# A planned kernel of linear attention and an MLP: code-block boundaries in the planner, early products and norms off VectorE, some K transposed by DMA

## The chip, the cores and the metric

The kernel runs on one core of one Trainium2 chip. TensorE (PE) multiplies matrices; its weight loads are shown as a row of their own (PEld). VectorE (DVE), ScalarE (ACT) and GpSimd (POOL) work on elements, SyncE (SP) issues most of the DMAs, and 16 DMA engines move the data. The metric is the device time of one execution in microseconds (us), less is better. Times are medians over executions; the profile is of one execution.

## What is computed

The reference is a linear attention with a delta rule over 768 steps for 4 x 8 heads of width 48, and then an MLP with a tanh gelu on the 3072 tokens.

```
k_n = k / (norm(k, axis=-1) + 1e-06)
for t in range(S):
    y[:, :, t] = einsum('bhd,bhde->bhe', q[:, :, t], state)
    v_old = einsum('bhde,bhd->bhe', state, k_n[:, :, t])
    state = state + beta_t * einsum('bhd,bhe->bhde', k_n[:, :, t], v[:, :, t] - v_old)
x = y.transpose(0, 2, 1, 3).reshape(3072, 384)
out = gelu_tanh(x @ w_in) @ w_out          # 384 -> 2048 -> 384
```

## The kernel before

**A planner writes the order.** The kernel doesn't loop over instructions in a fixed order. Each piece of work is declared with `op(...)`: which engines can do it and what it should cost there, what it reads and writes, a priority (less is more urgent), the number `nm` of matmuls in it, and for a DMA its semaphore. `Plan.schedule` (L110) then simulates the engines with these costs and picks, for each engine, the next operation: one that could start within `NEAR` of the engine's free time goes before one that is late, and among these the most urgent. The result is five fixed instruction streams (`emit`, L268). An engine executes its stream strictly in order and waits with semaphores, so where real times differ from planned ones, an engine waits in its place. SP's and POOL's DMAs stand in their streams like all else.

**Code blocks.** PE's stream has some 11,000 instructions, a weight load and a matmul for each of 5446 matmuls. They are fetched in blocks of 256. Class `Fetch` (L32) models that: each time PE's count passes a multiple of 256, the next block must have arrived, which takes TIME = 3.7 us after the crossing before, or BUSY = 6.5 in the first 50 us. A PE operation that would stall longer than `SLACK` counts as late by the rest (L194 to L199).

**Stages.** The 768 steps are cut into 12 chunks of 64, two chunks to a unit. Heads lie in pairs on 128 partitions, 16 pairs side by side. For a chunk:
- `prep` (L670) squares K (`sq`), sums it (`ss`, L682, a VectorE reduce), and makes 1/norm (`rn`); `prep2` (L739) scales K to `Kn` on POOL or VectorE, transposes it on PE with 8 matmuls against an identity (L762) and copies the result to `KQT` (L773). `prepq` (L715) does the like for Q (L728).
- `gram` (L775) multiplies K with K and with Q. ScalarE copies the first to `G`; VectorE multiplies the second by the decay mask `mD` into `DT` (L800).
- `own` (L804) and `blocks` (L834), once a unit: a triangular 16x16 inverse by a recurrence of 14 steps, each a product into `tmp` and a sum into `Yf` (L872, L876). For unit 0 it runs on VectorE, for later units on POOL. `XW`, `TB` (L891), then in `inverse` (L896) `WB` and `DI` (L917), `ET`, and three `TT` steps widen it to 64x64.
- `state` (L979): R, U, the new state S and the outputs of a chunk, copied to `x4` (L1076).

`mlp` (L1082) works on tiles: tile 0 is chunk 0, tile 1 is chunk 1, the others are two chunks each. SP moves some rows of x first, six small DMAs a tile (not for tile 0). The first layer's results go through gelu on ScalarE to `gT`, the second layer's to `osb` and out by SP. Only banks 6 and 7 of PSUM are used by MLP work until the last tile.

**Loads.** K, V and Q chunks are loaded on SP (`load`, L565). The weights are loaded on POOL's queue: W1 and W4 (the parts of w_in) after chunk 2 of K has landed, W2 (w_out) after the first Qs. `O` (L357) holds the priorities.

Of the kernel before, what the change touches and what calls it, by code (L numbers as in the profile page):

```python
# [17 lines left out]
URGENT = -100.0  # L18
EARLY_T, MARGIN = 55.0, (2.0, 1.0, 0.2)
# [12 lines left out]
class Fetch:  # L32

    BLOCK, TIME, BUSY, BUSY_T = 256, 3.7, 6.5, 50.0

    def __init__(self):
        self.pos, self.ready = 0, 0.0

    def run(self, t, cost, n, keep=False):
        pos, ready = self.pos, self.ready  # L40
        per = cost / n
        while n:
            k = min(self.BLOCK - pos % self.BLOCK, n)
            t += k * per
            pos += k
            n -= k
            if pos % self.BLOCK == 0:
                t = max(t, ready)
                ready = t + (self.BUSY if t < self.BUSY_T else self.TIME)
        if keep:  # L50
            self.pos, self.ready = pos, ready
        return t
# [7 lines left out]
class Plan:  # L60
# [49 lines left out]
    def schedule(self):  # L110
# [51 lines left out]
        while n_left:  # L162
            pick = None
            for e in ENGINES:
# [3 lines left out]
                for i in ready[e]:  # L168
# [34 lines left out]
                    far = late > (NEAR[e] if o.prio > URGENT else 0.12)  # L203
# [19 lines left out]
            if o.dma:  # L223
                arrival = o.end + 1.5
                if e == "pool":
                    w_free = max(arrival, w_free) + o.bw
                    o.lat = w_free + 0.5 - o.end
                    for p in queued:
                        if p.end + p.lat - 0.5 > arrival:
                            p.lat += o.bw  # L230
                    if dma_free > arrival:
                        dma_free += o.bw
                        dep_cache.clear()
                    else:
                        dma_free = w_free
                else:
                    dma_free = max(arrival, dma_free) + o.bw
                    o.lat = dma_free + 0.5 - o.end
                    queued.append(o)
# [28 lines left out]
    def emit(self):  # L268
# [64 lines left out]
        with nc.Block() as blk:  # L333
# [19 lines left out]
GATE = 2  # L353
XQ_, OQ_ = "sp", "sp"
BURST, SLACK = 0.6, 0.15
NEAR = dict(pe=0.2, dve=0, act=0.2, pool=0.5, sp=0.0)
O = dict(step=79.0, prepq=-76.8, prep=-99.5, prep0=-83.8, prep1=-94.9, prep2=-81.3, gram=-57.3, w2=-63.2,  # L357
         prepq0=-58.2, dt0=-84.0, dtb=-43.9, dt=-67.0, own=-153.9, own0=-86.2, blk0=-78.6, inv0=-95.4,
         st0=-103.2, own1=-46.4, blk=-48.3, blk1=-29.7, invb=-46.3, stb=-46.9, inv=-22.2, st=24.3,
         x=23.8, mlpa=-100, m1=1.6, m2=53.1, outs=300, ldq=-122.7, ldk=-121.8, ldv=-92.0)  # L360
# [50 lines left out]
def bass_deltanet__then__act_gelu_tanh_kernel(  # L411
# [25 lines left out]
    with nc.allow_non_contiguous_dma("head rows"), nc.allow_low_precision("bf16 matmuls"):  # L437
# [127 lines left out]
        def load(nm, c, pr):  # L565
# [11 lines left out]
            for a in range(2):  # L577
                op({"sp": 0.75}, {"sp": f_dma(t[s][64 * a:64 * a + 64, :, :], sv[a, C * c:C * c + C, :, :])},
                   reads=after, writes=[f"{nm}{s}_{a}"], prio=pr, dma=f"d_{nm}{c}", bw=1.27)
# [6 lines left out]
        def load_w1(kt, pr):  # L586
            after = ["kf2_0", "kf2_1"]
# [9 lines left out]
        def load_w1x(pr):  # L597
            after = ["vf1_0", "vf1_1"]
# [13 lines left out]
        def load_w4(pr):  # L612
            op({"pool": 0.9}, {"pool": lambda e: e.memset(W4, 0.0)}, writes=W4S, prio=-96)
            after = ["kf2_0", "kf2_1"]
# [9 lines left out]
        def load_w2(j, pr):  # L624
            op({"pool": 0.8}, {"pool": f_dma(W2[:, 4 * j:4 * j + 4, :], w2v[:, 4 * j:4 * j + 4, :])},
               reads=["qf_0", "qf_1", "qf_2", "qf_3"],
               writes=[f"W2{j}"], prio=pr, dma=f"d_W2{j}", bw=2.5)
            bulk.append([f"W2{j}"])
# [7 lines left out]
        load("kf", 0, -70)  # L636
        for dup in range(2):
            op({"sp": 0.65}, {"sp": f_dma(BL[:, :, dup, :], bfl)}, writes=[f"BL{dup}"], prio=-69, dma="d_BL", bw=0.4)
# [11 lines left out]
        op({"pe": 1.0}, {"pe": f_mms(bt_mms)}, mode="m", bk="f", nm=3, reads=["BL0", "BL1", "identF"],  # L650
# [19 lines left out]
        def prep(c):  # L670
# [3 lines left out]
            parts = [slice(0, 8), slice(8, 16)] if c == 0 else [slice(0, NP)]  # L674
            for n, u in enumerate(parts):
# [6 lines left out]
                op({"dve": 0.95 * w}, {"dve": lambda e, u=u: e.tensor_reduce(ss[j][:, u], sq[:, u, :], AX.X, ALU.add)},  # L682
                   reads=[f"sq{n}"], writes=[f"ss{j}{n}"], prio=pr)
# [31 lines left out]
        def prepq(t):  # L715
            pr = O['prepq0'] + 5 * t if t < 2 else T(2 * t, O['prepq'])
# [22 lines left out]
        def prep2(c):  # L739
# [3 lines left out]
            parts = [slice(0, 8), slice(8, 16)] if c == 0 else [slice(0, NP)]  # L743
            for n, u in enumerate(parts):
# [3 lines left out]
                op({"dve": 0.9 * w} if c == 0 and n == 0 or c == 1 else {"pool": 1.5 * w}, {"pool": f, "dve": f},  # L748
                   reads=kn + [f"rn{j}", f"Kz{i}"], writes=[f"K{i}_{n}"] if len(parts) == 2 else [f"K{i}_0", f"K{i}_1"], prio=pr)
            tn = (kts(c),)  # L750
            for kk, (t, rd) in enumerate(((Kn[i], [f"K{i}_0", f"K{i}_1"]),)):
# [23 lines left out]
        def gram(c, g):  # L775
            i, r_ = c % RB, c % RT
            pr = T(c, O['gram'] + 2 * g)
# [17 lines left out]
            def gview(kk):  # L795
# [4 lines left out]
            op(d_ps(512), {"dve": lambda e: e.tensor_tensor(  # L800
                pv(DTb[r_][:, ps_, :]), gview(1)(), mD[:, :].unsqueeze(1).unsqueeze(1).to_broadcast([128, 2, 4, C]),
                ALU.mult)}, reads=[h] + MD, writes=[f"DT{r_}_{g}"], prio=pr + O['dt'] if c > 1 else O['dt' + '0b'[c]])
# [176 lines left out]
        def state(c):  # L979
# [94 lines left out]
            if c > 0:  # L1074
# [3 lines left out]
               reads=[ho], writes=[f"x{t % NX}_{hf}"], prio=pr + O['x'])  # L1078
# [67 lines left out]
        for kt in range(KT):  # L1146
            W1N += load_w1(kt, -62 + kt)
        W4N = load_w4(-59)
# [3 lines left out]
           writes=["warm2"], prio=O["prep1"] + 1)  # L1152
# [62 lines left out]
```

## Time and profile before

| What | us |
|---|---|
| median of 13 runs | 266.24 |
| lowest and highest | 261.72, 272.84 |
| the profiled execution, its own time | 266.75 |
| its span, from the first to the last instruction | 265.0 |
| busy in it: PE | 227.7 |
| busy: PE weight loads | 148.2 |
| busy: VectorE | 154.6 |
| busy: ScalarE | 153.5 |
| busy: GpSimd | 113.3 |

"Busy" is the time in which an engine executes at least one instruction. Matmuls overlap in PE's pipeline, so a busy PE need not run at its peak. The largest groups of work on each engine, with the busy time in us, then the mean in ns of one, then the idle time before them and who ended most of it:

```profile
L380 PE MATMUL ps<-x,W 128*128 128x512 bf16 (+1 forms) x336 | 75.7, 363 | 2.5 <-issue 2.3
L380 PE MATMUL ps<-W,gT 128*128 128x384 bf16 x384 | 66.9, 327 | 0.0
L373 ACT ACTIVATE gT<-ps 128x512 bf16<-128x512 f32 x96 | 57.2, 597 | 50.8 <-PE ps L380 48.0
L876 POOL TENSOR_TENSOR Yf<-Yf,tmp 128x28 f32<-128x28 f32 (+6 forms) x70 | 24.8, 354 | 5.5
L800 DVE TENSOR_TENSOR DT<-ps,mD 128x512 bf16<-128x512 f32 x24 | 16.3, 686 | 8.2 <-ACT G L373 8.0
```

The first two rows are the two layers of the MLP; nearly all other matmuls are short ones of attention. A line such as L380 or L364 is that of a helper which emits many different operations, so the names of the tiles tell which one it is.

### The profile page before, as it was taken

Reading aid. Unit: us, or ns where it says so; the run is one execution under the profiler, and the core shown is the slowest. Engines: PE = TensorE matmul, PEld = TensorE weight load, DVE = VectorE, ACT = ScalarE, POOL = GpSimd, SP = SyncE. Lnnn points to the kernel's source line nnn. Section 1 sums busy time; section 2 is a strip of 40 time slices with the busy share of each in tenths; the row PEclk is TensorE's granted clock in tenths of the full one; section 3 lists DMA queues with packets and bytes.
Section 4 is the critical chain, followed back from the end, with each engine's and each line's share of the span. In section 5 each row is a group of like instructions: output and inputs, shape, how many; then the busy total and the mean of one; then the engine's idle time right before and its main releaser. Section 6 shows DMA issues by size and latency. Waiting matters only on the chain.

```text
span 265.0 us, 11874 instructions
## 1 busy us (share of the span) xinstructions
PE 227.7 (86%) x5446; PEld 148.2 (56%) x5446; DVE 154.6 (58%) x274; ACT 153.5 (58%) x257; POOL 113.3 (43%) x213
## 2 busy tenths in 40 slices
PE   0655277699949999899998998999999999999995
PEld 0544277477737766465675646666556564456462
DVE  5778993577543688688997849457695120002011
ACT  4489368469706899669731678363655605960600
POOL 8279309889028880588604884078500000000000
PEclk9999999999985999999999999999999999999999
DMA  6999999961794308753350130311100012001102
GB/s 124 217 172 219 182 186 138 191 139 37 153 173 102 62 15 182 189 121 59 78 126 32 36 63 20 62 35 35 62 17 5 2 50 86 0 0 62 59 34 84
DMA packets 65009, 23.91 MB, mean 90 GB/s; under 512 B 52736, under 2 KB 64480, under 8 KB 64960
## 3 DMA queue, kind: packets, MB, share of 16 engines
q1 hardware_dynamic: 62208, 19.62, 35.0%
q0 software_dynamic: 2752, 3.54, 8.1%
q8 instruction: 42, 0.69, 1.1%
q14 instruction: 7, 0.06, 0.1%
HBM read 21.43 MB, written 4.72 MB: 99 GB/s over the span
## 4 chain that ended last, share of the span: by engine, by line
PE 63%; DVE 12%; POOL 12%; ACT 6%; issue 6%; POOLq 0%
PE ps L380 60%; POOL Yf L876 4%; POOL tmp L872 4%; DVE TB L891 2%; PE ps L728 2%; DVE WB L917 2%; PE ps L762 2%; ACT KQT L373 2%; POOL XW L882 1%; POOL Yf L867 1%; DVE ss L682 1%; DVE Tt L857 1%; DVE ET L364 1%; DVE TT L364 1%; DVE DI L917 1%
## 5 line engine op out<-in xcount | busy, mean ns | idle before, releaser
L373 ACT ACTIVATE gT<-ps 128x512 bf16<-128x512 f32 x96 | 57.2, 597 | 50.8 <-PE ps L380 48.0
L380 PE MATMUL ps<-x,W 128*128 128x512 bf16 (+1 forms) x336 | 75.7, 363 | 2.5 <-issue 2.3
L380 PE MATMUL ps<-W,gT 128*128 128x384 bf16 x384 | 66.9, 327 | 0.0
L380 PEld LDWEIGHTS ps<-W,gT 128*128 128x128 bf16 x384 | 35.7, 98 | 23.5 <-ACT gT L373 0.3
L380 PEld LDWEIGHTS ps<-x,W 128*128 128x128 bf16 x336 | 30.7, 102 | 28.2 <-issue 2.5
L369 DVE COPY osb<-ps 128x384 f32<-128x384 f32 x17 | 9.5, 558 | 51.5 <-PE ps L380 51.2
L364 DVE TENSOR_TENSOR TT<-ps,DI 128x256 bf16<-128x256 f32 (+4 forms) x39 | 24.9, 646 | 22.6 <-PE ps L380 22.2
L380 PE MATMUL ps<-KQT 48*32 48x32 bf16 (+1 forms) x1152 | 18.9, 202 | 10.4 <-issue 5.8
L373 ACT ACTIVATE KQT<-ps 128x1024 bf16<-128x1024 bf16 (+1 forms) x24 | 23.8, 1002 | 5.7 <-PE ps L762 4.6
L876 POOL TENSOR_TENSOR Yf<-Yf,tmp 128x28 f32<-128x28 f32 (+6 forms) x70 | 24.8, 354 | 5.5
L867 POOL TENSOR_TENSOR Yf<-Tt,bM 128x512 f32<-128x512 f32 x5 | 6.4, 1276 | 47.2 <-DVE Tt L857 35.3
L872 POOL TENSOR_TENSOR tmp<-Yf 128x28 f32<-128x28 f32 (+6 forms) x70 | 24.1, 344 | 5.4
L380 PEld LDWEIGHTS ps<-KQT 48*32 48x32 bf16 (+1 forms) x1152 | 13.9, 99 | 15.7 <-issue 8.1
L380 PEld LDWEIGHTS ps<-TT,ET 64*64 64x64 bf16 x768 | 15.8, 116 | 10.2 <-issue 4.1
L800 DVE TENSOR_TENSOR DT<-ps,mD 128x512 bf16<-128x512 f32 x24 | 16.3, 686 | 8.2 <-ACT G L373 8.0
L380 PE MATMUL ps<-TT,ET 64*64 64x32 bf16 (+1 forms) x768 | 18.4, 182 | 3.0 <-issue 1.6
L364 POOL TENSOR_TENSOR Kn<-kf,rn 128x768 bf16<-128x768 f32 (+1 forms) x11 | 17.2, 1579 | 2.8 <-DVE rn L692 2.8
L373 ACT ACTIVATE G<-ps 128x512 bf16<-128x512 f32 x24 | 14.0, 596 | 7.3 <-PE ps L380 7.2
L891 DVE STREAM_TRANSPOSE TB<-XW 128x512 f32<-128x512 f32 x12 | 12.6, 1049 | 3.3 <-POOL XW L882 3.3
L373 ACT ACTIVATE x<-ps 128x1024 bf16<-128x1024 f32 x12 | 12.3, 1023 | 3.2 <-PE ps L380 2.7
L364 DVE TENSOR_TENSOR R<-ps,vf 128x768 bf16<-128x768 f32 x11 | 10.4, 948 | 5.9 <-PE ps L380 5.9
L373 ACT ACTIVATE U<-ps 128x768 bf16<-128x768 f32 x12 | 9.8, 813 | 7.0 <-PE ps L380 6.8
(96 smaller groups left out, 306.6 us busy)
## 6 DMA issues: line engine op xcount, KB each, us to landing
kf<-in_k_dram SPq DMA_DIRECT2D x24, 192.0 KB, 4.4
qf<-in_q_dram SPq DMA_DIRECT2D x24, 192.0 KB, 4.3
vf<-in_v_dram SPq DMA_DIRECT2D x24, 192.0 KB, 4.4
out_dram<-osb SPq DMA_DIRECT2D x20, 192.0 KB, 1.9
W<-in_moe_w_in_dram POOLq DMA_DIRECT2D x8, 192.0 KB, 6.5
W<-in_moe_w_out_dram POOLq DMA_DIRECT2D x4, 384.0 KB, 8.9
out_dram<-osb SPq DMA_DIRECT2D x8, 96.0 KB, 3.3
x<-x SPq DMA_DIRECT2D x30, 16.0 KB, 1.8
```

The source lines that it names most:

```text
L364: return lambda e: e.tensor_tensor(out() if callable(out) else out, a() if callable(a) else a, b() if callable(b) else b, op)
L369: return lambda e: e.tensor_copy(out, a() if callable(a) else a)
L373: return lambda e: e.activation(out, a() if callable(a) else a, func)
L380: ins = t.matmul(out, lhsT, rhs, start=st, stop=sp_, skip_group_check=skip)
L728: ins = e.transpose(o[:, a, j], Qn[:, n, a, j, :, :].rearrange("q h d -> q (h d)"), identB[:, :])
L762: ins = e.transpose(tb()[:, m, :], t[:, 2 * m:2 * m + 2, :].rearrange("p h d -> p (h d)"), identB[:, :])
L800: op(d_ps(512), {"dve": lambda e: e.tensor_tensor(pv(DTb[r_][:, ps_, :]), gview(1)(), mD[:, :].unsqueeze(1).unsqueeze(1).to_broadcast([128 ...
L867: sb_op(256 * nb, lambda e: e.tensor_tensor(Yv(), tv_, bm, ALU.mult), [f"Tt{j}", bmn], [YN], 0, [(hY, 1)] if inp else ())
L872: sb_op(nb * s * w, lambda e, s=s, w=w, tv=tv: e.tensor_tensor(tv, yf[:, :, s:s + 1, 0:s].to_broadcast([128, nb, w, s]), Yv()[:, :, s + 1: ...
L876: sb_op(nb * s * w, lambda e, s=s, tv=tv: e.tensor_tensor(Yv()[:, :, s + 1:16, 0:s], Yv()[:, :, s + 1:16, 0:s], tv, ALU.add), [YN, f"tmp{j ...
L891: op({"dve": 1.05}, {"dve": lambda e, w=w: e.transpose(TB[w].rearrange("q (n j) -> q j n", j=16), XW[w].rearrange("q x b i -> q x (b i)")) ...
L917: op(dict(d_ps(48 * n), act=3 * (0.18 + 0.0133 * n)) if c < 4 else d_ps(48 * n), {"act": on_act, "dve": lambda e, g=g, n=n: e.tensor_tenso ...
```

## The change

It has these parts:
- `Fetch` starts its count at 63, so that the first boundary comes after 193 instructions; each operation's count is multiplied by 1.0025; the time of a block is 6.5 us until 50 us, 4.5 until 125, and 3.7 after. `SLACK` goes from 0.15 to 0.3. The matmuls that transpose beta are counted as 12.
- In the choice of the next operation, those more urgent than CRIT = -85 may be waited for 0.4 us on their engine. `NEAR` and all priorities in `O` are new, some with another form for chunk 0.
- The decay products DT of chunks 0 and 1 become a copy on ScalarE and a product on POOL. The row sums of squares of chunks 2 and 3 are folded on POOL in six adds. Chunk 1's preparation is cut in two halves as chunk 0's was.
- K of chunks 8 to 11 is transposed by one DMA each, issued on SP, in place of 8 matmuls and a ScalarE copy.
- Half of the first K load and one of the two beta loads are issued on ScalarE's queue. W1 and W4 wait for chunk 0 of K, no longer for chunk 2, and are more urgent. Three loads get an earliest planned time.

```diff
 class Fetch:
-    BLOCK, TIME, BUSY, BUSY_T = 256, 3.7, 6.5, 50.0
+    BLOCK, FIRST, EVENTS = 256, 63, 1.0025
+    TIMES = ((50.0, 6.5), (125.0, 4.5), (1e9, 3.7))
...
-        self.pos, self.ready = 0, 0.0
+        self.pos, self.ready = float(self.FIRST), 0.0
...
-                ready = t + (self.BUSY if t < self.BUSY_T else self.TIME)
+                ready = t + next(w for x, w in self.TIMES if t < x)
...
-                    far = late > (NEAR[e] if o.prio > URGENT else 0.12)
+                    far = late > (NEAR[e] if o.prio > URGENT else 0.12 if o.prio > CRIT else WAIT)
...
-                        if p.end + p.lat - 0.5 > arrival:
+                        if p.end + p.lat - 0.5 > arrival + 1.5:
...
+CRIT, WAIT = -85.0, 0.4
+NPE = 8
-BURST, SLACK = 0.6, 0.15
-NEAR = dict(pe=0.2, dve=0, act=0.2, pool=0.5, sp=0.0)
+BURST, SLACK = 0.6, 0.3
+NEAR = dict(pe=0.2, dve=0.2, act=0.05, pool=0.5, sp=0.0)
...
-                op({"sp": 0.75}, {"sp": f_dma(t[s][64 * a:64 * a + 64, :, :], sv[a, C * c:C * c + C, :, :])},
-                   reads=after, writes=[f"{nm}{s}_{a}"], prio=pr, dma=f"d_{nm}{c}", bw=1.27)
+                en = "act" if (nm, c, a) == ("kf", 0, 1) else "sp"
+                op({en: 0.75}, {en: f_dma(t[s][64 * a:64 * a + 64, :, :], sv[a, C * c:C * c + C, :, :])},
+                   reads=after, writes=[f"{nm}{s}_{a}"], prio=pr, dma=f"d_{nm}{c}" + (f"_{a}" if c == 0 and nm == "kf" else ""), bw=1.27,
+                   at={("kf", 4): 19.0, ("vf", 2): 20.0, ("kf", 5): 21.0}.get((nm, c), 0.0))
...
-            after = ["kf2_0", "kf2_1"]
+            after = ["kf0_0", "kf0_1"]
...
-            parts = [slice(0, 8), slice(8, 16)] if c == 0 else [slice(0, NP)]
+            parts = [slice(0, 8), slice(8, 16)] if c < 2 else [slice(0, NP)]
...
+                if c in (2, 3):
+                    for z in (24, 12, 6, 3):
+                        op({"pool": 0.2 + 1.65e-3 * 16 * z}, {"pool": f_tt(sq[:, :, 0:z], sq[:, :, 0:z], sq[:, :, z:2 * z], ALU.add)},
+                           reads=["sq0"], writes=["sq0"], prio=pr)
+                    op({"pool": 0.23}, {"pool": f_tt(ss[j][:, :], sq[:, :, 0], sq[:, :, 1], ALU.add)},
+                       reads=["sq0"], writes=[f"ss{j}0"], prio=pr)
+                    op({"pool": 0.23}, {"pool": f_tt(ss[j][:, :], ss[j][:, :], sq[:, :, 2], ALU.add)},
+                       reads=["sq0", f"ss{j}0"], writes=[f"ss{j}0"], prio=pr)
...
+            if c >= NPE:
+                op({"sp": 1.0}, {"sp": f_dma(KQT[i][:, 0, :, :], Kn[i].rearrange("p n d -> p (n d)"), True)},
+                   reads=[f"K{i}_0", f"K{i}_1"], writes=kts(c), prio=pr + 0.2, dma=f"d_T{c}", bw=2.5)
+                return
...
+            if c < 2:
+                op({"act": 0.6}, {"act": f_act(dv, gview(1))}, reads=[h], writes=[dn], prio=pr + 0.8)
+                op({"pool": 1.05}, {"pool": f_tt(dv, dv, md, ALU.mult)}, reads=[dn] + MD, writes=[dn], prio=dp)
+            else:
+                op(d_ps(512), {"dve": lambda e: e.tensor_tensor(dv, gview(1)(), md, ALU.mult)}, reads=[h] + MD,
+                   writes=[dn], prio=dp)
```

Left out are the new numbers in `O` (all of them change; `step`, the spacing of priorities from chunk to chunk, goes from 79.0 to 72.6, gelu's `mlpa` from -100 to 0, `outs` from 300 to -100), and the same edit of a weight load in two more places.

## The prediction

> **What bounds the kernel now.** I read first where each engine is busy along the span, then the stages around the start, then the chain of waits, then the waits by engine.
>
> ```profile
> PE   0655277699949999899998998999999999999995
> PEclk9999999999985999999999999999999999999999
> DMA  6999999961794308753350130311100012001102
> q8 instruction: 42, 0.69, 1.1%
> ```
>
> From slice 8 on (about 50 us) PE is at 8 or 9 nearly everywhere. Before that it is at 2 to 7, while the DMA engines stand at 9: the first 50 us are a start-up in which the loads and a serial attention chain run. The dip to 5 in PEclk is a stretch at half clock (about 79 to 86 us in this execution, some 3.4 us of work); I expect it in both kernels. The q8 line is the fetching of instructions, in 16 KB blocks.
>
> ```profile
> 40.00:50.00 10.00, 6.53 (x183) 5.69 (x182) 3.14 (x5) 7.18 (x10) 8.96 (x19) 1.00 1.05 158
> 50.00:60.00 10.00, 9.73 (x204) 7.22 (x203) 7.51 (x20) 5.56 (x10) 8.78 (x18) 1.00 0.85 159
> 220.00:240.00 20.00, 20.00 (x102) 9.70 (x100) 1.12 (x2) 14.33 (x24) 0.00 (x0) 1.00 0.03 11
> ```
>
> After the stretch come busy times of PE, weight loads, VectorE, ScalarE, GpSimd, then the clock and the DMA share. The last 54 us (208 to 262) hold MLP matmuls alone. The last x is copied at 211.4 us and one MLP tile takes about 20 us, so some 30 us of MLP work is in hand when attention ends: the attention chain can be late without moving the end. What moves the end, one for one, is the moment at which PE becomes full (49.1 us, the first MLP matmul), what PE stands idle after it, and how much work it has.
>
> ```profile
> 17.95 1.02 ACT KQT L373
> 24.67 1.29 DVE DT L800 x2
> 25.96 0.18 DVE tmp L872
> ...
> 31.70 0.56 DVE WB L917
> ...
> 46.61 2.11 issue
> 48.73 0.36 PE ps L380 x7
> ...
> 73.72 1.19 issue
> ...
> 76.72 2.30 issue
> ...
> 125.50 2.13 DVE WB L917
> ...
> 134.99 1.00 PE ps L762 x16
> ...
> 138.93 1.48 issue
> ```
>
> The chain of waits shows two things. Until 44 us it is VectorE's serial chain for chunk 0, interrupted by DT. And it has stretches called "issue", in which PE waits for nothing that a semaphore tells.
>
> ```profile
> PE ps L380 <- issue: 13.2, 10, 3.1
> PE ps L380 <- DVE S L364: 0.8, 1, 0.8
> ```
>
> Of all PE's waits after 60 us, "issue" is 8.0 us and the next is 0.8. I counted PE's instructions (two for each matmul) in the trace up to each large "issue" gap: 705, 1473, 2753, 3009, 4545, 6337, 7105, 7873, 10177. All are 193 plus a multiple of 256. So these are waits for the next code block, and the first boundary lies at 193: what the new FIRST = 63 says (256 - 63 = 193), where the old model begins at 256.
>
> **The change, part by part.** The sum is made against the profiled execution (266.75 us, span 265.0), which is 0.5 us above the median of the 13 runs.
>
> *Block boundaries, stall times, SLACK.* The planner prefers a matmul group that does not stall over one that does. With boundaries misplaced by 63 it avoided stalls where there were none. The Trainium skill speaks against any gain here: "Runtime: NRT & Kernel Launch", section "Instruction fetch mechanics", holds that fetching is hidden because the sequencer issues more slowly than blocks arrive. By the page this part is worth 0; by the row, up to 8.0 us after 60 us and 2.1 at 46.6. The row decides: block fetches that followed each other at once began 3.5 to 4.3 us apart (107.5, 111.2, 115.4, 119.1), while 103 KQT matmuls at 138 us were through in 1.01 us, so that a block of such short ones (128 matmuls) lasts some 1.25 us. Stalls are avoidable only where MLP matmuls are at hand; after 60 us they are. The new time of 4.5 to 125 us is cautious against 3.8 to 4.3 measured there. I take half: 4.0 us (ends 0 and 7).
>
> *Off VectorE at the start.* Chunk 0's two decay products (0.69 + 0.68) and the reduces of chunks 2 and 3 (0.94 + 0.95) sit inside VectorE's 28-step recurrence. In VectorE's timeline the step after each starts late by 1.3, 0.8 and 1.05 us: 3.1 us. Chunk 1's products (36.6, 37.7) sit between the last TT steps: another 1.1. Sum 4.2 us on the chain to the first x. What is put elsewhere: ScalarE gets four evictions of 0.6 us; it waited 4.37 us for TB before 31.7, which covers them (without it 2.4 us go on the chain). GpSimd gets four products, nearest row bM 128x512 at 1.26 us, so 5.0 us; and for each of two chunks six small adds, by its own rows (0.25 to 1.3 us by size) about 2.9, so 5.8 together. It had 9.88 us idle before 39.85 and 4.45 before 14.04, and the weight loads that it issued from 16.5 to 27.4 (5.5 us) move into the early hole. It fits with some 3 us to spare.
> Here a second page speaks against the change: "SBUF — State Buffer", "Who interferes with whom": a VectorE instruction with two SBUF inputs and a GpSimd one that reads SBUF exclude each other for a whole instruction. The trace agrees: WB took 2.13 us at 125.5, beside two Kn on GpSimd, against 0.95 at 134.1, and 0.56 for the half-size one at 31.7 with GpSimd idle. In the new start WB and DI of chunk 0 can meet products on GpSimd; the steps of the recurrence have one input in PSUM and did not slow beside Kn at 19.8 us (0.23). One meeting costs up to 1.2. I take 0.7: the chain is 3.5 us shorter (without the page 4.2; with both meetings 1.8).
>
> *What is late next.* W1 landed by 35.1, W2's four parts at 48.4 to 55.9 (landing records), both before their use (second MLP layer from 63.3). W1's condition moves from kf2 to kf0, so its 2 MB go ahead of part of qf0, vf0, kf2 and kf3 on full DMA engines: up to 10 us later. qf0 and vf0 have that slack (G is used at 32, U at 41); kf2 and kf3 (15.98, 19.37) have about as much, not more. Code blocks are another limit: in the start they came 5 to 8 us apart (fetches at 27.0, 33.4, 38.4, 46.3), and six lie before the first MLP matmul, so the 2.1 us stall at 46.6 is not also gained. For the whole start I take 3.5 us (ends -3 and 6). Half of kf0 and one BL from ScalarE's queue: kf0's second half lands up to 0.8 earlier, but GpSimd's tables end only at 6.16, so 0 to 0.6; ScalarE waits 2.8 us there for kf anyhow. The split of chunk 1's preparation, and bt's count of 12, I cost at 0 (+-0.3): both lie before 17 us beside the chain.
>
> *K of chunks 8 to 11 by DMA.* Gone: 32 transposes on PE, in two groups of 1.07 and 1.23 us with their tail, 2.0 us of PE, and four ScalarE copies of 1.02, hidden. Added: four DMAs on SP. None such is in the trace. Below: x<-x, SBUF to SBUF, 16 KB, 1.8 us; above: a kf load of 192 KB, 4.4 us; I take 4.4, as these move 256 KB. K of 9 is ready at 129 and its transposes ran only at 135, so KQT comes earlier than now; K of 11 is ready at 161.75 and its copy ended at 166: even. Each waits on SP for GpSimd's Kn; behind it stand vf loads, x moves and stores. The x moves of 128.7 and 160.8 could be some 2 us late; the 20 us of second-layer work then in progress covers it (uncovered, 4 us in all). Value 2.0 (ends -2 and 2.3).
>
> *All priorities, NEAR, WAIT, CRIT, at and queue rules.* The whole order is drawn anew. An urgent operation may hold an engine up to 0.4 us; with a few per chunk that is 1 to 3 us of PE, of which part replaces waits such as DVE S (0.8). I take a loss of 1.2 (ends -4 and 3).
>
> Sum: -4.0 -3.5 -2.0 +1.2 = -8.3 us: 266.24 - 8.3 = 258.
>
> **The rivals.**
> 1. *The start gives nothing* (loads and code blocks bind it: DMA at 9 to 46 us speaks for it; that PE at 45.4 had x0 and W1 and still ran something else speaks against). Then 2 to 2.5 us from stalls and 2 from transposes remain, about 262, from 260.5 to 265.
> 2. *Slower: GpSimd in the first 40 us.* Unit 1's recurrence begins on GpSimd at 39.85 and runs 18 us; every later unit follows it. If kf2 and kf3 land 10 us late and 10.8 us of new work stands before it, it starts at 45 or later. Between 63 and 100 us PE lives on tiles 0 and 1 alone (about 22 us of matmuls) and attention of these chunks. So each us beyond about 3 is idle PE: 6 late plus stalls that return, 272, from 269 to 280. Against: the moved weight issues free 5.5 us; for: the sum of work leaves only 3.
> 3. *It doesn't do what it says*: stalls are avoided by the plan but its times drift by more than a block's slack, and come back elsewhere, eating the start's gain: 266, from 264 to 268.5.
>
> **How the numbers follow.** Forecast 0.49 (252 to 261), rival 1 0.15 (two thirds of it below 263.6), rival 3 0.12, rival 2 0.24. One per cent, 2.7 us, is about what a measurement of this kernel can tell from no change (its 13 runs go from 261.72 to 272.84). Faster 0.49 + 0.10 = 0.59; same 0.05 + 0.12 = 0.17; slower 0.24. The range 252.5 to 270.5 leaves out about 0.05 below and 0.15 above; the forecast's own range is 252 to 261.
>
> **What would show it.** Right: the first 128x256 MLP matmul at 44 to 47 us; no DT and two fewer ss on VectorE before 30 us; PE's "issue" after 60 us near 4 us; attention's last x no later than 220; L762 with 64 matmuls instead of 96. Wrong: GpSimd's first Yf after 43 us with idle PE between 60 and 100; "issue" still 8 us; or PE waiting for KQT from a DMA after 125 us.

## The result, and the profile after

| | before | changed |
|---|---|---|
| median, us | 266.26 (48 runs) | 262.54 (11 runs) |
| lowest, highest | 261.72, 272.84 | 260.78, 263.84 |
| the profiled execution, its span | 266.75, 265.0 | 261.79, 260.0 |

The ratio changed / before is 0.9926, interval 0.9893 to 0.9960; run again later (e16), the changed kernel gave 262.23 and 0.9845 (0.9774 to 0.9917). The ratios take only executions within 1.5% of their kernel's fastest, which leaves 14 of the 48 of before, so the first ratio lies nearer to 1 than the medians (0.986). The changed kernel is faster, by 0.7 to 1.6%; 3.1% were forecast (258.0).

Ahead of a closer reading, two views of the changed kernel, to be held against those of before. First the busy tenths in 40 slices, and a DMA queue:

```profile
PE   0563455799898999998899999999999999999995
PEclk9995575559999999999979999999999999999999
DMA  8999899982389636783039130310100021001112
q10 hardware_dynamic: 1440, 0.30, 0.6%
```

From slice 8 on PE is as full as before. The start still takes seven and a half slices, with the DMA engines at 8 or 9; q10 is new, the queue of the DMA transposes. The 5s in PEclk up to 57 us are not new: the trace of the kernel before has no record of the clock ahead of 54.2 us, and its 128x256 MLP matmuls took 421 ns (median) until then, as long as those of the changed kernel at a clock of 0.5, and 273 ns at full clock. Then the waits of PE after 60 us (us in total, times, longest), the largest of the kernel before and the largest three of the changed one:

```profile
PE ps L380 <- issue: 8.0, 8, 2.3
...
PE ps L388 <- issue: 2.0, 3, 1.2
PE ps L388 <- ACT x L381: 1.3, 1, 1.3
PE ps L388 <- DVE ET L372: 1.2, 2, 0.6
```

"Issue" went from 8.0 us to 2.0, and waits for other engines from 1.4 to over 4. To see where the sum failed, I split each span from the first 128x256 MLP matmul to the end of the last one: PE's gaps, then the loss at half clock (half of the time that MLP matmuls ran at a clock of 0.5; ahead of a trace's first clock record, half of the time in which they took 421 ns), then the rest, which is work. Each column is one execution.

| us | before | changed | difference | forecast |
|---|---|---|---|---|
| first MLP matmul | 49.10 | 49.01 | -0.1 | -3.5 |
| gaps "issue" | 8.14 | 2.88 | -5.3 | -4.0 |
| gaps, waits for others | 2.07 | 4.90 | +2.8 | +1.2 |
| half clock | 4.05 | 3.15 | -0.9 | 0 |
| rest | 198.69 | 197.15 | -1.5 | -2.0 |
| end of the last MLP matmul | 262.04 | 257.08 | -5.0 | -8.3 |

Of the 3.3 us that are missing the start is 3.4. The chain of waits of the changed kernel shows the last 21 us of the start (start, length, what ran):

```profile
27.80 1.12 POOL DT L372
28.92 1.44 POOL Kn L372
...
30.41 1.05 PE ps L785 x8
...
31.48 1.02 ACT KQT L381
...
36.95 1.76 issue
38.71 3.74 PE ps L388 x100
42.45 2.74 issue
45.19 0.47 PE ps L388 x6
...
48.04 0.92 ACT x L381
...
49.01 1.03 PE ps L388 x4
```

Two things hold it that were not there before in this form: K of chunk 3, which comes from GpSimd only at 30.41, behind the folds and a decay product; and two waits for code, 4.5 us together, between 37 and 45 us.

**A correction.** Description and prediction say that W1 and W4 wait for chunk 0 of K, earlier than before. The name `kf0_0` is a buffer's. When `load_w1` is called, chunk 3 has been declared into it too, so W1 waits for chunk 3, later than before (it landed at 19.01, chunk 2 in the kernel before at 15.98). The rest of the delay is GpSimd's order: the issues stand behind the folds, both Kn and two decay products. The trace has the w_in parts here:

```profile
31.41 3.30 POOL L396 DMA_DIRECT2D W<-in_moe_w_in_dram  x6
```

In the kernel before they began at 16.47. Their last part lands at 45.95, not 35.06.

### The profile page after: what moved, and what is told of

Same layout as the page of the kernel before. It is cut to its first block, busy times and chain, and to the rows that moved or that the text cites. A ratio compares the mean times of both kernels' runs of the same rounds, so it can differ in the third digit from the quotient of the medians.

```text
span 260.0 us, 11830 instructions
## 1 busy us (share of the span) xinstructions
PE 223.2 (86%) x5414; PEld 144.3 (55%) x5414; DVE 157.0 (60%) x273; ACT 145.7 (56%) x248; POOL 129.8 (50%) x233
## 4 chain that ended last, share of the span: by engine, by line
PE 56%; POOL 16%; DVE 13%; issue 6%; ACT 4%; SPq 2%; DMA 2%; POOLq 0%
PE ps L388 55%; POOL Yf L906 4%; POOL tmp L902 4%; DVE WB L947 3%; POOL Kn L372 3%; POOL sq L372 3%; DVE TB L921 2%; SPq L396 2%; DMA qf<-in_q_dram 2%; DVE DI L947 2%; POOL XW L912 1%; DVE DT L831 1%; POOL Yf L897 1%; PE ps L747 1%; ACT KQT L381 1%
## 5 line engine op out<-in xcount | busy, mean ns | idle before, releaser
L388 PE MATMUL ps<-x,W 128*128 128x512 bf16 (+1 forms) x336 | 74.6, 357 | 3.8 <-issue 2.1
L388 PE MATMUL ps<-W,gT 128*128 128x384 bf16 x384 | 67.8, 329 | 0.5 <-issue 0.5
L388 PEld LDWEIGHTS ps<-x,W 128*128 128x128 bf16 x336 | 29.5, 100 | 29.9 <-ACT gT L381 4.1
L381 ACT ACTIVATE KQT<-ps 128x1024 bf16<-128x1024 bf16 (+1 forms) x20 | 19.6, 982 | 11.1 <-PE ps L747 6.4
L372 POOL TENSOR_TENSOR Kn<-kf,rn 128x768 bf16<-128x768 f32 (+1 forms) x12 | 19.2, 1608 | 5.2 <-DVE rn L727 3.2
L388 PEld LDWEIGHTS ps<-TT,ET 64*64 64x64 bf16 x768 | 15.0, 113 | 9.1 <-issue 5.0
L388 PE MATMUL ps<-TT,ET 64*64 64x32 bf16 (+1 forms) x768 | 17.4, 180 | 2.5 <-issue 1.8
L831 DVE TENSOR_TENSOR DT<-ps,mD 128x512 bf16<-128x512 f32 x20 | 13.6, 684 | 7.1 <-ACT G L381 6.7
L897 POOL TENSOR_TENSOR Yf<-Tt,bM 128x512 f32<-128x512 f32 x5 | 6.4, 1282 | 21.6 <-DVE Tt L887 21.6
L947 DVE TENSOR_TENSOR DI<-TB,mB 128x768 bf16<-128x768 f32 (+1 forms) x13 | 14.2, 1096 | 0.1
L372 DVE TENSOR_TENSOR ET<-ps,mE 128x768 bf16<-128x768 f32 (+1 forms) x10 | 9.1, 914 | 6.2 <-PE ps L388 6.1
```

Of the source, the lines that this page charges most:

```text
L372: return lambda e: e.tensor_tensor(out() if callable(out) else out, a() if callable(a) else a, b() if callable(b) else b, op)
L381: return lambda e: e.activation(out, a() if callable(a) else a, func)
L388: ins = t.matmul(out, lhsT, rhs, start=st, stop=sp_, skip_group_check=skip)
L831: op(d_ps(512), {"dve": lambda e: e.tensor_tensor(dv, gview(1)(), md, ALU.mult)}, reads=[h] + MD, writes=[dn], prio=dp)
L897: sb_op(256 * nb, lambda e: e.tensor_tensor(Yv(), tv_, bm, ALU.mult), [f"Tt{j}", bmn], [YN], 0, [(hY, 1)] if inp else ())
L947: op(dict(d_ps(48 * n), act=3 * (0.18 + 0.0133 * n)) if c < 4 else d_ps(48 * n), {"act": on_act, "dve": lambda e, g=g, n=n: e.tensor_tenso ...
```

## The experiments

In e1 to e4, e12 and e18 the planner draws a new order. In all others the changed kernel's five orders are kept, and single operations are taken out, put elsewhere or exchanged, so that nothing else moves.

**The parts alone.** e1 is the kernel before with the new `Fetch`, e2 the changed one with the old, e3 without DMA transposes, e4 the kernel before redrawn:

```diff
 e1, e2 (reversed)
-    BLOCK, TIME, BUSY, BUSY_T = 256, 3.7, 6.5, 50.0
+    BLOCK, FIRST, EVENTS = 256, 63, 1.0025
 ... (TIMES, SLACK and the count of 12 go with it)
 e3
-NPE = 8
+NPE = 12
 e4
-O = dict(step=79.0, ...
+O = dict(step=78.5, ...
```

> The kernel before with the new block model alone (FIRST, EVENTS, TIMES, SLACK, the count of 12); the order is drawn anew, nothing else differs. Theory S (the boundaries bring the gain, and what followed it in the full change took most of it back): PE's issue waits after 60 us fall from 8.0 to 3 us or less, and the time falls by 3 to 6 us, to 260 to 263. Theory R (any redrawing of the order moves the time by some us, and the boundaries are one draw more): the issue waits fall too, but other waits of PE after 60 us grow by as much, and the time lies at 264 to 268.

> The changed kernel with the old block model (first boundary after 256, 3.7 and 6.5 us, SLACK 0.15). Theory S: PE's issue waits after 60 us come back, from 2.0 to 6 us or more, and the time rises by 3 to 6 us over the changed kernel, to 265 to 268. Theory R: no fixed sign, 260 to 268, and the issue waits don't tell the time.

> The changed kernel with K of chunks 8 to 11 transposed on PE again. If PE is the bound there and the transposes were its work, 2.0 us come back: 264 to 265. If the wait for ACT x at 129 us (1.26 us) and the half clock behind it come from the DMA way, the time stays at 262 to 263. More than 266 would be the redrawn order.

> A control: the kernel before with the spacing of priorities from chunk to chunk at 78.5 in place of 79.0, nothing else. It measures what a redrawn order is worth by itself. Theory R: 2 us or more in either direction from 266. Theory S: within 1.5 us of 266, with issue waits after 60 us of 6 to 10 us.

| | us | ratio to before | "issue" gaps | waits | rest |
|---|---|---|---|---|---|
| e1 | 267.25 | 1.0064 (1.0014 to 1.0115) | 0.88 | 9.45 | 201.29 |
| e2 | 269.65 | 1.0172 (1.0072 to 1.0272) | 4.77 | 9.16 | 197.40 |
| e3 | 266.25 | 1.0084 (1.0035 to 1.0132) | 2.99 | 6.18 | 199.54 |
| e4 | 268.14 | 1.0128 (1.0047 to 1.0209) | 4.90 | 6.51 | 199.37 |

(The three columns on the right are of one traced execution; for e2 it took 271.77.) e1 took 7.3 us of code waits away and gave all back. PE's waits in it after 60 us:

```profile
PE ps L384 <- DVE DT L804: 2.9, 3, 1.5
PE ps L732 <- DVE S L368: 2.3, 1, 2.3
PE ps L766 <- DVE DT L804: 2.1, 1, 2.1
```

As I read it, the stalls had hidden chains of VectorE that were just in time. So the boundaries are where the new model puts them, and here they paid only together with the other numbers. e2 points the same way from the other side, +7 us. e3 against the changed kernel is 3.7 us longer: rest +2.4, waits +1.3; the transposes are worth about their PE time (forecast 2.0). But e4 warns: a redrawn order of the kernel before costs 1.3% with no part changed. The control for the changed kernel, step 72.2 for 72.6, came last:

> The changed kernel with step 72.2 for 72.6: the same parts, the order drawn anew, a control for the runs in which the planner drew a new order (old Fetch, no DMA transposes, weights after chunk 0). If the order itself is tuned as finely as in the kernel before (a like redrawing cost that one 1.3%): 264 to 267. If its order isn't special: 261.5 to 263.5.

It took 261.36 (0.9873, 0.9828 to 0.9917), no slower than the changed kernel. So its order doesn't look special, and the losses of e2 (7.1 us) and e3 (3.7) exceed what either redrawing cost (e4: 1.8 by the medians). With one redrawing of each kernel, a share of them can still be the redrawing's.

**The start: GpSimd's sums, decay products, W2.** e5 makes one VectorE reduce of the six folds again, in chunk 2 and in chunk 3; e6 issues W2 later; e7 puts the decay products back on VectorE; e8 is e5 and e6, with W1 issued right behind bM.

```diff
 e5: the folds of chunks 2, 3
-pool: 6 x tensor_tensor(sq.., add) -> ss
+dve:  tensor_reduce(ss, sq, add)
 e6: order of GpSimd
-..., W4, W20..W23, DT1, Yf, tmp, Yf, ...
+..., W4, DT1, Yf, tmp, ... (8 tmp) ..., W20..W23, tmp, ...
 e7: chunks 0, 1
-act: copy -> DT ; pool: DT * mD
+dve: ps * mD -> DT
```

> The changed kernel with its order kept instruction by instruction, but for the sums of squares of chunks 2 and 3: the six adds on GpSimd are one VectorE reduce again, at the place where the squares are due. Theory G (the start gained nothing because GpSimd became its bound): K of chunk 3 is ready some 4 us earlier, PE's waits for it (2.56 and 2.74 us) shrink to under 1.5 each, and the first MLP matmul comes at 45 to 47 us in place of 49.0; time 259 to 261. Theory C (code blocks bind the start): PE reaches 30 us earlier but stands longer at the next block boundaries; first MLP matmul at 48 to 49.5, time 262 to 263. If VectorE's chain is still the bound, two reduces of 0.95 put it 1 to 2 us later: 263 to 265.

> The changed kernel with its order kept, but for the four w_out loads, issued in the middle of GpSimd's first recurrence (about 50 us) and no longer at 36.8. Theory C with the loads as its cause: a block's fetch starts 1 to 2.5 us after the boundary in place of 3.1 to 3.7 in 36 to 50 us, the three stalls of 1.76, 2.74 and 0.87 us shrink to under 3 us in all, and the first MLP matmul comes at 46 to 47.5 us; time 260 to 262. Theory G: the stalls stay or PE waits elsewhere, first MLP matmul at 48.5 to 49.5, time 262 to 264. GpSimd's recurrence runs 3 us longer for the issues in it, w_out lands by about 66 us, before 68.5.

> The changed kernel with its order kept, but for the decay products of chunks 0 and 1: one VectorE product each again, where the copies on ScalarE stood. By the prediction these four products cost VectorE's chain 2.4 us: first MLP matmul at 50 to 52 us, time 264 to 266. Theory G: GpSimd is relieved of 4.6 us in front of K of chunk 3 and of its first recurrence, and the start is no later: 47.5 to 49.5 us, time 261 to 263.

> The changed kernel with its order kept, with three edits: the reduces of chunks 2 and 3 on VectorE, the w_in loads issued ahead of chunk 2's squares on GpSimd (about 16 us, as in the kernel before), and the w_out loads in the middle of its first recurrence. From 36 to 50 us no bulk load is left. Theory C: stalls at block boundaries before the first MLP matmul fall from 5.4 us to under 2, and it comes at 44 to 46 us; time 257 to 260. Theory G alone: like the reduce edit by itself. If the five us of w_in issues put K of chunks 2 and 3 as late as the adds did, the first MLP matmul stays at 48 to 49 us.

e5 262.42 (0.9910, 0.9873 to 0.9947), e6 261.68 (0.9889, 0.9843 to 0.9935), e7 263.25 (0.9952, 0.9912 to 0.9993), e8 264.76 (0.9977, 0.9940 to 1.0013). With the sums back on VectorE (e5) the first MLP matmul came at 50.20, with the products back (e7) at 49.67: the two parts are worth 1.2 and 0.7 us at that place, each alone, and at most 0.7 us in the time. In e6 the two stalls before 45 us stayed (1.95 and 2.59) and the first MLP matmul came at 48.92; only the stall of 0.87 behind it was gone. So the W2 loads are not what makes the start late. In e5 K of chunk 3 still came at 30.4, because ScalarE's square root of that norm stands behind another copy in its fixed order; e5 could not test what it was made for.

e8 tells something else. Its waits of PE from 31 to 49.5 us have no "issue" line at all among the larger ones:

```profile
PE ps L785 <- POOL Kn L372: 2.5, 1, 2.5
PE ps L388 <- DVE TT L372: 2.3, 2, 1.9
PE ps L388 <- ACT KQT L381: 0.7, 1, 0.7
```

The code stalls of the start were gone, since the weights had landed by 36.4. But the price is in GpSimd's timeline: W1's issue waited 3.50 us for chunk 3 and held up the chain behind it.

```profile
19.33 3.29 POOL L396 DMA_DIRECT2D W<-in_moe_w_in_dram  x6 [3.50 <-DMA kf<-in_k_dram]
...
31.50 1.48 POOL L372 TENSOR_TENSOR Kn<-kf,rn 128x768 bf16<-128x768 f32 x1 [2.76 <-DVE rn L711]
```

**The norm chain, and a wait of 1.3 us at 130.** e9 is e5's sums and e6's W2, and the other steps of chunk 3's norm put ahead on ScalarE, VectorE and GpSimd. (W2 stands as in e6 in e10, e11, e13, e14, e15 and e17 too.) e10 is e6 with the ScalarE copy of chunk 5's x ahead of the two `TT` operations before it, e11 both.

```diff
 e9: order of ScalarE; of GpSimd
-..., copy KQT(2), sr(3), sr(3), ...  |  ..., DT0_0, Kn(3), DT0_1
+..., sr(3), sr(3), copy KQT(2), ...  |  ..., Kn(3), DT0_0, DT0_1
 e10: order of ScalarE at 128 us
-TT, TT, x(5)
+x(5), TT, TT
```

> The changed kernel with its orders frozen; only chunk 2's and 3's row sums become one VectorE reduce each, the two ScalarE steps of chunk 3's norm go ahead of the copy of chunk 2's K, VectorE's rn of chunk 3 goes directly behind its reduce, Kn of chunk 3 goes ahead of chunk 0's decay product on GpSimd, and the four W2 issues go to the ninth tmp of GpSimd's first recurrence. Theory N (what makes the start late is the norm chain of chunk 3, GpSimd first and then the order on ScalarE and VectorE): K of chunk 3 is transposed at about 28 instead of 30.4, the crossing at 705 comes at 31 instead of 33.2, the recurrence of chunk 0 has no step of over 0.9 us in it, the first MLP matmul is at 46 to 47.5 instead of 49.0, and the time is 259 to 260.5. Theory F (the fetching of code under load binds it): the crossings come earlier by 2 us but the stalls at 961 and 1217 grow by as much, the first MLP matmul stays at 48.5 to 49.5 and the time at 261 to 262.5.

> The changed kernel with its orders frozen; the W2 issues as in the run with W2 alone moved (261.68), and the copy of chunk 5's x goes ahead of the TT operations that stood before it on ScalarE and waited for TB. If new waits in PE's stream are what took a part of the gain: PE's wait of 1.26 us for ScalarE's x at 130 us is gone and with it the half-clock stretch of 3.4 us that followed at 132.4 (some 0.9 us of work); 0.9 to 2 us off against W2 alone, so 259.7 to 260.8. If that time is only handed on to a later wait (TT later by 0.5 us, the chain of the unit behind it): another wait of about 1 us within 10 us of the place, and 261.3 to 262.2.

> The two edits together (norm chain, W2, and chunk 5's x copy). Theory N and the wait as a true cost: 257.5 to 259.5, the sum of both gains. Theory F: 260 to 261.

e9 262.69, e10 262.33, e11 262.45, against 267.27 of the kernel before run beside them (ratios 0.9846, 0.9817, 0.9842, each +-0.005): none can be told from the changed kernel's 0.9845. In e9 K of chunk 3 was transposed at 28.20, 2.2 us earlier, and the crossing at 705 came at 31.73. The first MLP matmul came at 48.76, 0.25 earlier, less than two traces of the changed kernel differ (49.01, and 48.67 in e16). VectorE's timeline of e9 shows one half of why:

```profile
19.64 1.96 DVE L897 TENSOR_TENSOR ps<-Tt,bM 128x512 f32<-128x512 f32 x1
...
23.88 0.95 DVE L1249 TENSOR_REDUCE ss<-sq 128x16 f32<-128x768 f32 x1
...
33.59 2.86 DVE L947 TENSOR_TENSOR DI<-TB,mB 128x384 bf16<-128x384 f32 x2
```

The reduces are in the recurrence again, and L897 and `DI`, whose inputs are both in SBUF, took 1.96 and 2.86 us beside GpSimd's squares and decay products (0.69 and 1.03 alone). In e10's trace (an execution of 264.12) the wait for x at 130 was gone and others stood in its place:

```profile
PE ps L388 <- DVE S L372: 1.9, 1, 1.9
PE ps L388 <- DVE TT L372: 1.4, 1, 1.4
```

By the median, 262.33 against 261.68 of e6, nothing was gained: the second theory of its expectation held, the wait was handed on.

**Weights earlier.** e12 gives W1 and W4 the condition that the description had claimed, by a name that only the first load carries, with a redrawn order. e14 issues them behind bM at 16 us with the old condition, and reduces chunk 2 on VectorE to make room.

```diff
 e12
-            after = ["kf0_0", "kf0_1"]
+            after = ["first_0", "first_1"]
 e14: order of GpSimd
-bM, folds(2), sq(3), Kn(2), folds(3), DT0_0, Kn(3), DT0_1, W1, W4
+bM, W1, W4, sq(3), Kn(2), folds(3), Kn(3), DT0_0, DT0_1
```

> The changed kernel, but W1 and W4 wait for what the text of the change says, the first chunk of K, by a name of its own (the name used there is a buffer's, which chunk 3 fills again); order and times drawn anew by the planner. If the late weights are the cause of the late start (weights that land at 45.95 with x0 not far ahead, and late code under their load): W1 is issued before 13 us, lands before 36, the stalls at 961 and 1217 fall from 4.5 to under 2.5, first MLP matmul at 45 to 47, 258 to 260. If they take DMA share from the first loads of K, V and Q instead: kf2 and kf3 land 3 to 6 us later (over 19), the recurrence and K of chunk 3 follow them, first MLP matmul at 49 to 52, 263 to 267. A redrawn order alone cost the kernel before 1.3%, so up to 3 us of a loss are not evidence by themselves; the landings and stalls are.

> The changed kernel with frozen orders and W2's issues moved as before; chunk 2's sums become one VectorE reduce behind the two products before the recurrence, chunk 3's stay on GpSimd, Kn of chunk 3 goes ahead of chunk 0's decay product, and W1 and W4 are issued into the hole that this leaves on GpSimd, behind bM at 16 us, with the condition of the kernel before (chunk 2 of K landed). If the two limits are the norm chain and the late weights with the late code: W1 lands before 38 instead of 45.95, 961 to 1217 takes under 5.5 us instead of 6.5, K of chunk 3 is transposed at 28 to 29.5 instead of 30.4, the first MLP matmul is at 46 to 47.3, the time 259 to 260.5: better than both kernels. If not: W1's issues push GpSimd's sq of chunk 3 past 22 and K of chunk 3 to 30.5 or later, and the first MLP matmul is at 48.5 or later, 261.5 to 263.

e12 274.75 (1.0261, 1.0183 to 1.0338), e14 266.49 (1.0016, 0.9974 to 1.0058). In e12 W1 went at 6.89 and landed by 26.84, and the second part of chunk 2 of K, at 15.99 before the edit, landed at 28.17. In e14 that load stayed early, W1 landed by 31.32, and Q of tile 1 landed at 34.52, not 24.56. Its waits of PE from 20 to 50 us:

```profile
PE ps L747 <- ACT Qn L381: 4.7, 1, 4.7
PE ps L785 <- POOL Kn L372: 4.7, 2, 2.5
...
PE ps L388 <- issue: 0.4, 1, 0.4
```

In both the DMA engines are nearly full for the first 35 us. Whatever of the loads goes first, another chain waits for the one that goes last; in the changed kernel the last are the weights.

**One limit or several.** e13 leaves the row sums of chunks 2 and 3 out on every engine. e15 is e13 with e14's early weights. e17 is e13 with GpSimd's decay products of chunk 1 behind VectorE's DI. e16 is the changed kernel again, told above.

```diff
 e13: chunks 2, 3 (the norm is then a rough number)
-pool: 6 x tensor_tensor(sq.., add) -> ss
+pool: tensor_tensor(sq[:, :, 0], sq[:, :, 1], add) -> ss
 e17
+DT1_0, DT1_1 on pool wait for DI0 on dve
```

> The changed kernel with frozen orders, W2's issues moved to the ninth tmp of GpSimd's first recurrence as before, and the row sums of squares of chunks 2 and 3 left out: one add of two columns on GpSimd in place of six each, and a constant in the norm, so K of these chunks is scaled by a wrong number; chunk 3's norm steps and Kn go ahead where their inputs are then ready. VectorE gets nothing for it. This is what the part could give if the sums cost no engine anything. If the start has one limit (the sums, wherever they stand): K of chunk 3 is transposed before 27.5, the recurrence takes under 11.3 us instead of 12.8, the crossing at 705 comes at 30 or before, the first MLP matmul at 45.5 to 46.5, and the time is 258.5 to 260. If code under the load of the weights is a second limit of the same size: the step from the crossing at 961 to that at 1217 still takes 6 us or more, and the first MLP matmul stays at 47.5 to 49, the time at 261 to 262.5.

> As the run with the sums left out, and W1 and W4 behind bM with chunk 2's condition as well. Both limits gone: 961 to 1217 takes under 5 us, the first MLP matmul is at 44 to 46, which is the 3.5 us that were forecast for the start, and the time is 257 to 259. If the first MLP matmul is earlier by 3 us and the time is not (260.5 or more), then the start doesn't pay one for one and something later sets the end.

> The changed kernel itself with no edit, for the other three of this call: 262.5 on a chip like the first; what it differs from that is the difference between calls, which is to be taken off before the runs of different calls are compared. All theories expect the same.

> As the run with the sums left out (e13), and the two GpSimd decay products of chunk 1 wait for VectorE's DI of chunk 0, so that the two no longer meet (DI took 3.37 us beside them there, 1.03 in the changed kernel). If VectorE's slowed DI was the third limit: DI is back at 1.0 to 1.1, the first DI,ET group on PE comes 1.5 us earlier, and the first MLP matmul at 46.0 to 47.3 instead of 48.45. If code is what remains: the crossing at 961 comes at 37.5 or earlier, 961 to 1217 grows to 6 us or more with a stall of 2 us, and the first MLP matmul stays at 47.8 to 48.5. The time is within 1 us of that run's 261.93 in both cases, since S of chunk 0 is only one of the things that the MLP's first tile waits for.

e13 took 261.93 (0.9833, 0.9767 to 0.9898), e15 266.34 (1.0015, 0.9969 to 1.0060), e17 260.69 (0.9866, 0.9803 to 0.9929). e15 ran into the late Q as e14 did. Neither of the others differs from the changed kernel by more than its own two ratios do from each other. In e13 chunk 3's K came at 27.79, and then VectorE's DI met the decay products:

```profile
33.31 3.37 DVE L947 TENSOR_TENSOR DI<-TB,mB 128x384 bf16<-128x384 f32 x2
```

e17 took that meeting away: DI was back at 1.03 us and the crossing at 961 came at 37.27, 1.4 earlier than in the changed kernel. PE's timeline of e17 shows what was left (start, length, group, idle before it):

```profile
37.27 0.86 PE L388 MATMUL ps<-TT,ET 64*64 64x32 bf16 x25 [0.17 <-issue]
...
40.94 0.83 PE L388 MATMUL ps<-R,TT 64*64 64x48 bf16 x23
44.29 0.46 PE L388 MATMUL ps<-R,TT 64*64 64x48 bf16 x9 [2.52 <-issue]
...
48.11 0.82 PE L388 MATMUL ps<-x,W 128*128 128x256 bf16 x3 [0.81 <-ACT x L381]
```

The 23rd and the 24th matmul of one group are 2.52 us apart: the group crosses a code block. The table puts the runs together. "Fetch" is the time from the crossing at 961 to the first packet of the next block, from the records of queue q8.

| us | W1 landed | crossing at 961 | fetch after it | crossing at 1217, of it stalled | first MLP |
|---|---|---|---|---|---|
| before | 35.06 | 36.93 | 1.45 | 41.40, 0 | 49.10 |
| changed | 45.95 | 38.71 | 3.70 | 45.19, 2.74 | 49.01 |
| changed again (e16) | 45.89 | 38.38 | 3.91 | 44.85, 2.25 | 48.67 |
| e8 | 36.39 | 39.85 | 1.04 | 44.13, 0 | 49.54 |
| e9 | 44.62 | 38.73 | 3.72 | 44.93, 1.90 | 48.76 |
| e13 | 43.40 | 38.66 | 2.59 | 44.33, 1.08 | 48.45 |
| e14 | 31.32 | 42.16 | 1.06 | 46.22, 0 | 51.61 |
| e17 | 42.78 | 37.27 | 3.69 | 44.29, 2.52 | 48.11 |

While the weights are still landing the block's first packet comes late, and the step to 1217 takes 5.7 to 7.0 us; where they have landed it takes 4.1 to 4.5. So the start has several limits close behind each other. Lifting the norm chain moved the first MLP matmul by 0.25 us (e9), the sums on every engine 0.56 (e13), the meeting at DI as well 0.90 (e17), counted from 49.01; from e16's 48.67 it is 0.34 less each, so only e17 is clear of that. Each time another wait held it.

## Why the prediction was right in direction and too large

**Right.** The bound on PE; the boundaries at 193 plus multiples of 256 (in the changed kernel PE crosses at 705, 961, 1217 as before); the stalls, -5.3 against -4.0, within the ends; the transposes, -1.5 against -2.0. Their DMAs took longer than the value of 4.4 and none was waited for:

```profile
L395 SPq DMA_TRANSPOSE KQT<-Kn x4: 1247/1513/3271, 110.4 to 137.5; - x4
...
DMA to landing us min/median/max: 4.3/5.0/5.3
```

**The step that failed** is "For the whole start I take 3.5 us"; the traces showed 0.1, and 0.4 in e16. It summed what left VectorE's chain as if that chain alone set the first x. Four of its supports did not hold.

First, "the weight loads that it issued from 16.5 to 27.4 (5.5 us) move into the early hole": they moved the other way, to 31.4: I misread a buffer's name as a chunk's, and GpSimd's order put the new work ahead of them. "It fits with some 3 us to spare" rested on that.

Second, VectorE's recurrence took 12.84 us from Tt to its end, instead of the 10.6 that the removal promised (13.74 less 3.1):

```profile
18.19 1.43 DVE L896 TENSOR_TENSOR Yf<-Tt,bM 128x512 f32<-128x512 f32 x1
19.54 1.08 DVE L897 TENSOR_TENSOR ps<-Tt,bM 128x512 f32<-128x512 f32 x1
...
28.33 0.25 DVE L711 RECIPROCAL rn<-sr 128x16 f32<-128x16 f32 x1 [1.15 <-ACT sr L709]
```

The first two lines are the meeting with GpSimd that I priced at 0.7 and looked for at WB and DI: it came at L896 and L897 (1.13 us more than 0.69 each), beside the very folds that had been moved to spare VectorE. In the third, 1/norm of chunk 3 stands in VectorE's stream and waited 1.15 us for a square root on ScalarE, which had waited for GpSimd's sums; the recurrence stood behind it. Work taken off an engine came back as a wait in its stream.

Third, "the split of chunk 1's preparation, and bt's count of 12, I cost at 0 (+-0.3): both lie before 17 us beside the chain". Chunk 1's preparation is on the chain: its product of K with K is the last input of Tt, with which the recurrence begins. Chunk 1's sum, the square root behind it and Tt, in the kernel before and then in the changed one, where only the second half of the sum is shown:

```profile
9.75 0.95 DVE L682 TENSOR_REDUCE ss<-sq 128x16 f32<-128x768 f32 x1 [0.84 <-ACT sq L373]
10.74 0.21 ACT L373 ACTIVATE sr<-ss 128x16 f32<-128x16 f32 x1 [0.52 <-DVE ss L682]
15.44 1.25 DVE L857 STREAM_TRANSPOSE Tt<-ps 128x1024 f32<-128x1024 f32 x1 [1.48 <-PE ps L380]
...
11.50 0.55 DVE L701 TENSOR_REDUCE ss<-sq 128x8 f32<-128x384 f32 x1
12.67 0.20 ACT L381 ACTIVATE sr<-ss 128x16 f32<-128x16 f32 x1
16.90 1.25 DVE L887 STREAM_TRANSPOSE Tt<-ps 128x1024 f32<-128x1024 f32 x1 [1.77 <-PE ps L388]
```

The second half's sum stood behind other VectorE work, and the square root behind ScalarE's copy of Q. Tt began 1.46 us later, so the recurrence, though 0.9 us shorter, ended 0.56 us later than before (29.74, not 29.18). Whether the split or the new priorities put them there no run tells: all that keep the changed kernel's order have this late Tt (16.8 to 17.1).

Fourth, code. I named blocks as "another limit" in the start and gave them no price. The late weights gave them one: 4.5 us of stall between 37 and 45.

Rival 1, that the start gives nothing, is what happened: it named loads and code blocks as the cause, and its 262 is the measured time. I gave it 0.15. The number is partly luck: it had 2 to 2.5 us from stalls, and the runs had 5.3, of which new waits took 2.8. Of rival 2 the cause was there (GpSimd, K of chunk 3 late) and not the size: GpSimd began its first recurrence at 42.05, not at 45, and PE had work from 60 to 100.

**Mis-sized.** The new waits, +2.8 against +1.2; the largest is that for x at 130, ScalarE's order:

```profile
128.33 0.91 ACT L955 ACTIVATE TT<-TB,m 128x256 bf16<-128x256 f32 x2 [1.99 <-DVE TB L921]
129.15 1.00 ACT L381 ACTIVATE x<-ps 128x1024 bf16<-128x1024 f32 x1
```

x was ready and stood behind two copies that waited for a transpose. **Not in the sum:** I expected the half-clock stretch in both kernels as it stood; it came at another place, and half clock in all cost 0.9 us less. What sets it is open (below).

What stays open: no run had all limits lifted at once (early weights with Q and K in time), so what the start is worth then isn't shown. The new priorities, `NEAR` and the wait of 0.4 us were never run without the other parts, so their share isn't known. And no version here beats the changed kernel by more than the runs can tell; of those that compute the reference e18 (261.36) and e6 (261.68) have the lowest medians.

## What to carry to other kernels

A chain that gets shorter is worth only the distance to the next chain. Before a gain in a start-up is counted, write down when each other input of the same first instruction is ready: the loads, the code, each engine's part. Work that moves to another engine can come back as a wait in the stream that it left and as a slower neighbour. And a dependency by the name of a buffer is read with the last writer declared, not with the index in the name.

## What the runs showed of the hardware

- At the crossing at 961 the first packet of the next 16 KB code block came 1.04 to 1.45 us after PE crossed with the weights landed, and 2.6 to 3.9 while they were landing (the table). PE stalled at the next crossing in the runs of the second kind alone. So, as the table reads, a bulk load can stall PE without moving one byte that PE waits for.
- Some half-clock stretches followed waits of a microsecond or more. In the changed kernel the clock was 0.5 from 132.4 to 135.8, after the wait of 1.26 at 130; in the kernel before from 78.1 to 84.9, after stalls of 1.19 and 2.30; in e6, whose longest wait after 60 us was 1.2, there was no such stretch after 57.3. But the length of the wait doesn't decide: waits of 2.41 (e13, at 62) and 1.93 (e11, at 131) were followed by none, one of 1.18 (e9, at 62) was. That the wait is the cause was not tested by itself.
- `DI`, 1.03 us alone, took 2.86 and 3.37 beside GpSimd's decay products, and 1.03 again when these waited for it (e17).
